# Block-sparse attention with a maxout layer: v brought into the query-tile layout by engine copies instead of DMAs inside the chip

## The chip, the cores and the metric

The kernel runs on one NeuronCore of a Trainium2 chip. Its engines are TensorE (PE; its weight loads are listed as PEld), VectorE (DVE), ScalarE (ACT), GpSimd (POOL) and SyncE (SP, which issues the DMAs). The metric is the device time of one execution in microseconds. Three runs of the kernel before took 192.92, 193.31 and 194.15 us, so the median is 193.31.

## What is computed

```python
# B, H, S, D = 4, 8, 768, 64; block = 32, window = 16, nb = 24
k_sum = k.reshape(B, H, nb, block, D).max(axis=3)
v_sum = v.reshape(B, H, nb, block, D).mean(axis=3)
scores_l = scale * q @ k.T, kept where |i - j| < window     # local keys
scores_s = scale * q @ k_sum.T + log(block)                 # block keys
a = softmax(concat([scores_l, scores_s]))
attn = a @ concat([v, v_sum])                               # per batch and head
x = attn, heads side by side                                # 3072 x 512
out = maximum(x @ w1, x @ w2) @ w_out                       # d_ff = 1024
```

All inputs and the output are fp32; the matmuls run in bf16.

## The kernel before

The work of a batch is eight heads, taken as four pairs (hp), and 768 queries, taken as three groups (grp) of 256. The queries are cut into twelve tiles of 64. A query tile meets 128 keys only: 64 + 32 local keys around it and the 24 block keys (with fillers). So there is, for every query tile, a row block of values in `vx` (128 partitions x 12 tiles x 8 heads x 66): partitions 0 to 63 and 96 to 127 hold the 96 rows of v near the tile, partitions 64 to 95 hold the block means, the same in all twelve tiles, and column 64 holds ones, from which the softmax's sum comes.

How v gets into `vx` (`load_v`, lines 276 to 333) is what the change touches. v of one batch arrives in two DMAs of four heads each, as fp32, in `vf` (two buffers, 128 rows x 4 heads x 6 row blocks x 64). POOL casts each half to bf16 in `vb` (one buffer, L340 by way of the helper `copy`, labelled "cast v"). Five pieces move rows of `vb` to their partitions and tiles of `vx`: two of 64 partitions (even and odd tiles) and three of 32. In batches 1 to 3 all five are DMAs from SP (L304); in batch 0 the two large pieces are DVE copies (L340) and the three small ones DMAs. PE makes the block means by six matmuls of `amean` with `vb` (L313), DVE copies them into tile 0 of `vx` (L319), and a DMA from `vx` to `vx` spreads them to the other eleven tiles (L327). The ones travel along with the rows, since `vb` is 66 wide. The load of v for a batch is issued only when the copies of the batch before are issued (`behind`).

The rest of attention: k and q are loaded, cast (k on DVE, or POOL for three pairs of batch 0; q on ACT), turned by PE (L359) and placed (k by DVE L373 into `kx`, with the block maximum L375, the wrap L379 and the spread of the sums L382; q by ACT L388 into `qx`). PE computes scores (L414, in batch 0 with the mask added by L403), ACT takes the exponential into `pb` (L426), DVE multiplies by the mask in batches 1 to 3 (L435, L441), PE computes the values (L460: `pb` with `vx`), DVE divides (L472, L474), PE turns the result (L484) and DVE copies it to `xt` (L489).

The maxout layer uses max(a, b) = a + relu(b - a): DVE makes w2 - w1 (`wd`, L506), POOL casts w1 (`w1b`), PE turns it (L516) and multiplies it with w_out once (L544, `w1o`), so that for each group of 256 queries PE computes the hidden part (L560, relu by ACT L565), the linear part (L574) and the product of the hidden part with w_out (L581). ACT copies the result out (L340) and SP stores it.

The order on each engine is not written by hand. Every operation is recorded with its engine, an assumed cost, its inputs and buffers and a priority. `Plan.run` plays the whole kernel through with these costs and lets each engine take the ready operation of the highest priority. The order that results is then fixed: an engine waits in that order. A change of a cost or of a buffer therefore also moves operations that are not edited. `vx` has two buffers, taken in turn by batch 0, the turned w1 (`w1t`), and batches 1, 2 and 3.

Of the kernel before, what the change touches and what calls it, by code (L numbers as in the profile page):

```python
# [13 lines left out]
BF16 = mybir.dt.bfloat16  # L14
# [114 lines left out]
def kernel(  # L129
# [14 lines left out]
    nc = tc.nc  # L144
# [64 lines left out]
    def fixed_parts():  # L209
# [36 lines left out]
        def make_amean():  # L246

            nc.gpsimd.memset(amean[:], 0.0)
            am = amean[:, :, 64:64 + nb]
            nc.gpsimd.memset(am, 1.0 / block)  # L250
            for base, mult, pat in ((0, 1, [[128, NM], [-block, nb]]),
                                    (block - 1, -1, [[-128, NM], [block, nb]])):
                nc.gpsimd.affine_select(out=am, in_=am, compare_op=ALU.is_ge, fill=0.0, base=base,
                                        channel_multiplier=mult, pattern=pat)
            for t in vbr.slots:
                nc.gpsimd.memset(t[:, :, :, D:VW], 1.0)

# [15 lines left out]

    v_spread = {-1: []}

    def load_v(b, prio, engines):

        vb = Buf(vbr)
        for n in range(2):
            f = Buf(vfr)  # L280
            op("SP", 3.55, lambda f=f, n=n: nc.sync.dma_start(
                out=f.ap[:].rearrange("p h m d -> p (h m) d"),
                in_=v[b, 4 * n:4 * n + 4].rearrange("h (m r) d -> r (h m) d", r=128)),
               write=[f], behind=v_spread[b - 1], prio=prio, label=f"load v{b}{n}")
            copy(engines[n], 1536, lambda f=f, n=n: (
                vb.ap[:, :, 4 * n:4 * n + 4, 0:D].rearrange("p m h d -> p h m d"), f.ap[:]),
                 read=[f, amean_in], write=[vb], prio=prio + 1, label=f"cast v{b}{n}")

        def rows(t):
            return t.rearrange("p t h w -> p t (h w)")  # L290

        last = []
        for piece, (lo, hi, tiles_, part, ms) in enumerate((
                (0, 64, slice(0, NT, 2), 0, slice(0, NM)),
                (0, 64, slice(1, NT, 2), 64, slice(0, NM)),
                (96, 128, slice(0, NT, 2), 64, slice(0, NM)),
                (96, 128, slice(1, NT - 1, 2), 0, slice(1, NM)),
                (96, 128, slice(NT - 1, NT), 0, slice(0, 1)))):
            aps = lambda lo=lo, hi=hi, tiles_=tiles_, part=part, ms=ms: (
                rows(vx[b].ap[lo:hi, tiles_]), rows(vb.ap[part:part + hi - lo, ms]))  # L300
            kw = dict(read=[vb], write=[vx[b]], prio=prio + 2, label=f"spread v{b}{piece}")
            if engines[2][piece] == "SP":
                last.append(op("SP", (1.7, 1.6, 1.0, 0.85, 0.3)[piece], lambda aps=aps: (
                    lambda o, i: nc.sync.dma_start(out=o, in_=i))(*aps()), **kw))  # L304
            else:
                e = engines[2][piece]
                copy(e, 0, aps, us=(1, 1, 1, 5 / 6, 1 / 6)[piece] * {
                    "DVE": 1.75, "ACT": 2.4, "POOL": 3.1}[e], **kw)
        ps, s, mean = Buf(banks, "mm"), slice(64, 96), Buf(Ring([None]))

        def means():
            for m in range(NM):
                nc.tensor.matmul(out=bank(ps), lhsT=amean[:, m, :], rhs=vb.ap[:, m, :, 0:D],  # L313
                                 start=(m == 0), stop=(m == NM - 1))
# [8 lines left out]
        def spread_means():  # L323
            o, i = rows(vx[b].ap[s, 1:NT]), rows(vx[b].ap[s, 0:1])
            i = i.to_broadcast([32, NT - 1, H * VW])
            if engines[3] == "SP":
                nc.sync.dma_start(out=o, in_=i)  # L327
            else:
                nc.vector.tensor_copy(out=o, in_=i)

        t = op(engines[3], 1.5 if engines[3] == "SP" else 2.0, spread_means, read=[mean],
           write=[vx[b]], prio=prio + 2, label=f"spread means {b}")
        v_spread[b] = [*last, t] if engines[3] == "SP" else last

# [264 lines left out]
    FIRST = (("DVE", "ACT"), ("POOL", "ACT"), ("POOL", "ACT"), ("POOL", "ACT"))  # L599
    FIRST_SPREAD = ("DVE", "DVE", "SP", "SP", "SP")  # L600

# [23 lines left out]
    V0 = 0.5  # L625
    load_v(0, V0, ("POOL", "POOL", FIRST_SPREAD, "SP"))
    for hp in range(1, NP):
# [48 lines left out]
```

## Time and profile before

| what | value |
|---|---|
| median of three runs | 193.31 us (192.92 to 194.15) |
| span of the profiled execution | 192.5 us |
| PE busy | 166.4 us (86%) |
| DVE, ACT, POOL busy | 109.9 (57%), 114.1 (59%), 25.7 us (13%) |
| DMA queue 1 | 37.01 MB, 71.8% of 16 engines |
| DMAs vx<-vb | 18, median 7.8 us from issue to landing |
| mean granted clock of TensorE | 0.991 |

The page names a group of instructions by its line, engine, operation and tiles, with "x" and a count, then its busy time and the mean duration in ns, then the idle time of the engine just before these instructions and what ended it. In the timeline a row begins with the start and the duration in us; rows of several instructions are merged. A line can be that of a helper: L340 is every cast or copy recorded by `copy`, so the tile names tell what it is. The chain is the work that ended last, followed back from the end; it passes DMAs until 70 us and, but for 82 to 97 us, PE from there on.

### The profile page before, as it was taken

To read this page: it belongs to the slowest core of one execution; us is meant where nothing else is said; L and a number is where in the kernel's file an instruction comes from. 1 tells how busy PE (TensorE), PEld (TensorE's weight loads), DVE (VectorE), ACT (ScalarE), POOL (GpSimd) and SP (SyncE) were. 2 spreads that over 40 slices of the span, in tenths; PEclk is the share of its full clock that TensorE was granted. 3 is DMA by queue.
4 is the path that set the end of the run, shared out by engine and by line. 5 is a ranking of instruction groups with operands and counts; after the bars stand their busy time and mean duration, and the time that the engine had idled before them with its cause. 6 is when DMAs were issued, how large, how long until landed. Compare 5 with 4: busy or idle time off the path is not lost.

```text
span 192.5 us, 4148 instructions
## 1 busy us (share of the span) xinstructions
PE 166.4 (86%) x1643; PEld 117.9 (61%) x1664; DVE 109.9 (57%) x289; ACT 114.1 (59%) x173; POOL 25.7 (13%) x39
## 2 busy tenths in 40 slices
PE   0629619899999969999979999999999999999990
PEld 0426419865757738758657767487696676665740
DVE  6908956888979438759868953079777600000000
ACT  2533964384689949219967955179986443342621
POOL 7556221300330003300003300000000000000000
PEclk9999996999999999999999999999999999999999
DMA  5999999999999999999999996061020111120303
GB/s 187 226 305 356 234 240 347 371 381 281 210 359 251 292 268 217 339 309 217 229 288 223 340 218 193 3 164 24 3 109 5 54 58 59 50 109 0 112 0 109
DMA packets 47859, 37.27 MB, mean 194 GB/s; under 512 B 26208, under 2 KB 43744, under 8 KB 47840
## 3 DMA queue, kind: packets, MB, share of 16 engines
q1 hardware_dynamic: 47840, 37.01, 71.8%
q8 instruction: 13, 0.21, 0.5%
q14 instruction: 6, 0.05, 0.1%
HBM read 25.17 MB, written 6.29 MB: 163 GB/s over the span
## 4 chain that ended last, share of the span: by engine, by line
PE 53%; DMA 33%; SPq 5%; DVE 4%; POOL 2%; issue 1%; ACT 0%; ACTq 0%
PE banks L581 17%; PE banks L560 16%; DMA vf<-in_v_dram 13%; DMA vx<-vb 10%; PE banks L574 7%; PE banks L460 5%; DMA wf<-in_moe_w_out_dram 4%; SPq L503 4%; DMA vx<-vx 4%; PE banks L414 3%; DMA kqf<-in_k_dram 2%; PE banks L359 2%; POOL vb L340 2%; PE banks L484 2%; PE banks L313 1%; DVE pb L435 1%
## 5 line engine op out<-in xcount | busy, mean ns | idle before, releaser
L560 PE MATMUL banks<-xt,wd 128*128 128x256 bf16 x384 | 46.6, 273 | 0.5 <-DVE xt L489 0.5
L581 PE MATMUL banks<-wo,g 128*128 128x512 bf16 x184 | 44.9, 379 | 0.4
L560 PEld LDWEIGHTS <-wd 128*128 128x128 bf16 x384 | 36.4, 98 | 6.1 <-issue 0.7
L426 ACT ACTIVATE pb<-banks,bias 128x512 bf16<-128x512 f32 x48 | 31.5, 686 | 10.2 <-PE banks L414 9.9
L565 ACT ACTIVATE g<-banks 128x512 bf16<-128x512 f32 x48 | 28.3, 596 | 13.7 <-PE banks L560 13.2
L340 ACT COPY o<-banks 128x512 f32<-128x512 f32 x24 | 14.0, 585 | 28.7 <-PE banks L581 28.4
L388 ACT COPY qx<-banks 64x768 bf16<-64x768 bf16 x32 | 25.3, 791 | 6.1 <-PE banks L359 5.8
L581 PEld LDWEIGHTS <-g 128*128 128x128 bf16 x192 | 17.2, 97 | 16.5
L460 PE MATMUL banks<-vx,pb 128*128 128x65 bf16 x384 | 19.4, 196 | 3.6 <-DMA vx<-vx 1.8
L574 PE MATMUL banks<-w1o,xt 128*128 128x512 bf16 x85 | 21.9, 379 | 0.6
L460 PEld LDWEIGHTS <-pb 128*128 128x128 bf16 x384 | 16.9, 100 | 7.1 <-DMA vx<-vx 2.1
L359 PE MATMUL banks<-identity,kqb 128*128 128x128 bf16 x192 | 16.6, 234 | 5.3 <-DVE kqb L340 4.7
L340 ACT CAST kqb<-kqf 128x768 bf16<-128x768 f32 x16 | 13.1, 830 | 13.6 <-DMA kqf<-in_q_dram 8.7
L414 PE MATMUL banks<-qx,kx 128*128 128x128 bf16 (+2 forms) x208 | 18.6, 226 | 2.3 <-ACT qx L388 1.3
L340 POOL CAST vb<-vf 128x1536 bf16<-128x1536 f32 x8 | 12.2, 1520 | 55.0 <-DMA vf<-in_v_dram 35.2
L474 DVE TENSOR_TENSOR xs<-banks,inv 128x256 bf16<-128x256 f32 x48 | 19.1, 415 | 0.3
L414 PEld LDWEIGHTS <-kx 128*128 128x128 bf16 x208 | 15.1, 103 | 6.6 <-DVE kx L382 2.4
L359 PEld LDWEIGHTS <-kqb 128*128 128x128 bf16 x192 | 13.6, 106 | 8.5 <-DVE kqb L340 4.7
L373 DVE COPY kx<-banks 128x768 bf16<-128x768 bf16 x16 | 15.2, 955 | 2.9 <-PE banks L359 1.7
L375 DVE TENSOR_REDUCE ks<-kx 128x24 bf16<-128x768 bf16 x16 | 15.1, 944 | 0.1
L489 DVE COPY xt<-banks 128x512 bf16<-128x512 bf16 x24 | 9.8, 418 | 7.2 <-PE banks L484 6.8
L574 PEld LDWEIGHTS <-xt 128*128 128x128 bf16 x96 | 8.9, 98 | 7.9
(47 smaller groups left out, 129.8 us busy)
## 6 DMA issues: line engine op xcount, KB each, us to landing
kqf<-in_k_dram SPq DMA_DIRECT2D x16, 384.0 KB, 6.6
kqf<-in_q_dram SPq DMA_DIRECT2D x16, 384.0 KB, 5.7
vf<-in_v_dram SPq DMA_DIRECT2D x8, 768.0 KB, 10.7
out_dram<-o SPq DMA_DIRECT2D x20, 256.0 KB, 2.2
wf<-in_moe_w_dram SPq DMA_DIRECT2D x8, 512.0 KB, 11.1
vx<-vb SPq DMA_DIRECT2D x6, 396.0 KB, 8.0
wf<-in_moe_w_out_dram SPq DMA_DIRECT2D x4, 512.0 KB, 8.6
vx<-vx SPq DMA_DIRECT2D x4, 363.0 KB, 6.2
```

The source lines that it names most:

```text
L340: {"DVE": nc.vector.tensor_copy, "ACT": nc.scalar.copy, "POOL": nc.gpsimd.tensor_copy}[engine](out=o, in_=i)
L359: nc.tensor.transpose(out=bank(ps, S, BF16)[:, 128 * j:128 * j + 128], in_=src.ap[:, j].rearrange("p h d -> p (h d)"), identity=identity[:])
L373: op("DVE", 0.96, lambda: nc.vector.tensor_copy(out=kt()[:, :, 0:64], in_=order(kps)), read=[kps], write=[kx[b, hp], kmain], prio=prio, la ...
L388: op("ACT", 0.8, lambda a=a, r=r: nc.scalar.copy(out=qx[b, hp].ap[r, a, :], in_=order(qps)[r]), read=[qps], write=[qx[b, hp]], prio=prio, ...
L414: nc.tensor.matmul(out=o[:, :, n0:n1], lhsT=w, rhs=qx[b, hp].ap[:, :, c:c + n1 - n0], start=(mask_on != "PE"), stop=(mask_on != "PE" or (i ...
L426: op("ACT", 0.7, lambda: nc.scalar.activation(out=pv(), in_=bank(ps).rearrange("p (i w q) -> p i w q", w=2, q=64), func=ACT.Exp, bias=bias ...
L460: nc.tensor.matmul(out=av()[:, u, a, :], lhsT=pb.ap[:, 2 * u + a, 64 * par:64 * par + 128], rhs=vx[b].ap[:, 4 * grp + 2 * u + par, 2 * hp ...
L474: op("DVE", 0.42, lambda: nc.vector.tensor_tensor(out=x.ap[:, hp % 2], in0=av()[:, :, :, 0:D], in1=inv.ap[:].to_broadcast([128, 2, 2, D]), ...
L560: nc.tensor.matmul(out=bank(ps)[:, 256 * s:256 * s + 256], lhsT=wd[n].ap[:, c, 128 * s:128 * s + 128], rhs=x.ap[:, c, :], start=(c == 0), ...
L565: op("ACT", 0.6, lambda n=n, ps=ps: nc.scalar.activation(out=g.ap[:, 2 * n:2 * n + 2, :].rearrange("p f n -> p (f n)"), in_=bank(ps), func ...
L574: nc.tensor.matmul(out=bank(ps), lhsT=x.ap[:, c, sl], rhs=w1o[c].ap[:], start=(c == 0), stop=False)
L581: nc.tensor.matmul(out=bank(ps), lhsT=g.ap[:, f, sl], rhs=wo[f // 2].ap[:, f % 2, :], start=False, stop=(f == FC - 1))
```

## The change

The DMAs inside the chip go. `vb` becomes 64 wide and serves the means alone. Every piece is now an engine's cast from the fp32 `vf` into `vx`, per half of the heads, so ten pieces a batch in place of five. In batches 1 to 3 all ten are on POOL. In batch 0 DVE has five and POOL the other five. The ones are set by one POOL memset over all of `vx`. The means are spread by one DVE copy (32 partitions x 88 x 64), in all batches. The loads of v are no longer held behind the copies. In the new kernel's numbering lines are some 12 lower: L328 is the helper, L347 the turns, L304 the means, L310 their copy, L316 their spread, L402 the scores, L423 and L429 the masks, L448 the values, L548, L562 and L569 the maxout layer.

```diff
-    vbr = Ring(tiles("vb", 1, [128, NM, H, VW], BF16))
+    vbr = Ring(tiles("vb", 1, [128, NM, H, D], BF16))
...
-    def load_v(b, prio, engines):
+    def load_v(b, prio, casts, spreads, stretch):
 
         vb = Buf(vbr)
+
+        def piece(f, n, engine, to, of, tag, **kw):
+            aps = lambda: (vx[b].ap[to[0], to[1], 4 * n:4 * n + 4, 0:D].rearrange("p t h d -> p h t d"),
+                           f.ap[of[0], :, of[1], :])
+            count = 4 * D * len(range(NM)[of[1]])
+            copy(engine, 0, aps, us=0.1 + count * {"DVE": 0.00056, "ACT": 0.00102, "POOL": 0.00097}[engine],
+                 read=[f, *kw.pop("also", [])], write=[vx[b]], prio=prio + 1, label=f"spread v{b}{n}{tag}")
+
+        lo, hi, top, tail = slice(0, 64), slice(64, 128), slice(96, 128), slice(0, 32)
+        every = slice(0, NM)
...
-               write=[f], behind=v_spread[b - 1], prio=prio, label=f"load v{b}{n}")
+               write=[f], prio=prio, label=f"load v{b}{n}")
...
+            e = spreads[n]
+            piece(f, n, e[0], (lo, slice(0, NT, 2)), (lo, every), 0)
+            piece(f, n, e[1], (lo, slice(1, NT, 2)), (hi, every), 1)
+            piece(f, n, e[2], (top, slice(0, NT, 2)), (slice(64, 96), every), 2)
+            piece(f, n, e[3], (top, slice(1, NT - 1, 2)), (tail, slice(1, NM)), 3)
+            piece(f, n, e[3], (top, slice(NT - 1, NT)), (tail, slice(0, 1)), 4)
...
-        op("POOL", 0.1, lambda: nc.gpsimd.memset(vx[b].ap[s, 0, :, D:VW], 1.0),
-           write=[vx[b], mean], prio=prio, label=f"ones {b}")
+        op("POOL", 1.0, lambda: nc.gpsimd.memset(vx[b].ap[:, :, :, D:VW], 1.0),
+           write=[vx[b]], prio=prio, label=f"ones {b}")
...
+        def spread_means(lo, hi):
+            eng = nc.vector
+            eng.tensor_copy(out=vx[b].ap[s, lo:hi, :, 0:D], in_=vx[b].ap[s, 0:1, :, 0:D].to_broadcast(
+                [32, hi - lo, H, D]))
...
-    load_v(0, V0, ("POOL", "POOL", FIRST_SPREAD, "SP"))
+    load_v(0, V0, ("POOL", "POOL"), (("DVE", "DVE", "POOL", "POOL"), ("DVE", "DVE", "DVE", "POOL")), ((1, NT),))
...
-        load_v(b, 1000 * b - 480, ("POOL", "POOL", ("SP",) * 5, "SP"))
+        load_v(b, 1000 * b - 480, ("POOL", "POOL"), (("POOL",) * 4,) * 2, ((1, NT),))
```

Three places of the order matter below. The first is POOL in the prelude, from the arrival of the first half of v (`vf_92`) to the first weight cast. Before:

```order
L340 CAST vb_94<-vf_92 128x4x6x64
L340 CAST vb_94<-vf_93 128x4x6x64
L340 CAST kqb_70<-kqf_64 128x2x6x64
L340 CAST kqb_68<-kqf_66 128x2x6x64
L340 CAST kqb_69<-kqf_62 128x2x6x64
L340 CAST w1b_128<-wf_116 128x1024
```

And now:

```order
L328 CAST vb_94<-vf_92 128x4x6x64
L328 CAST vx_95<-vf_92 32x4x6x64
L328 CAST vx_95<-vf_92 32x4x5x64
L328 CAST vx_95<-vf_92 32x4x64
L328 CAST kqb_70<-kqf_64 128x2x6x64
L328 CAST vb_94<-vf_93 128x4x6x64
L328 CAST vx_95<-vf_93 32x4x5x64
L328 CAST vx_95<-vf_93 32x4x64
L328 CAST kqb_68<-kqf_66 128x2x6x64
L328 CAST kqb_70<-kqf_62 128x2x6x64
L328 CAST w1b_128<-wf_116 128x1024
```

Five casts into `vx` stand among the casts of k for pairs 1 to 3 (`kqb`), and one of these now comes ahead of the second half of v.

The second place is DVE in the prelude. Before, from the two copies of v to the placing of the last k (`kx_75`, the fourth pair):

```order
L340 COPY vx_95<-vb_94 64x6x528 x2
L373 COPY kx_73<-banks 128x12x64
L319 CAST vx_95<-banks 32x8x64
L375 TENSOR_REDUCE ks_98<-kx_73 128x24
L379 COPY kx_73<-kx_73 128x32
L382 COPY kx_73<-ks_98 128x12x24
L373 COPY kx_74<-banks 128x12x64
L373 COPY kx_75<-banks 128x12x64
```

And now, where two casts from `vf_92` stand five memsets ahead of the first row:

```order
L328 CAST vx_95<-vf_93 64x4x6x64 x2
L328 CAST vx_95<-vf_93 32x4x6x64
L361 COPY kx_73<-banks 128x12x64
L363 TENSOR_REDUCE ks_98<-kx_73 128x24
L367 COPY kx_73<-kx_73 128x32
L370 COPY kx_73<-ks_98 128x12x24
L310 CAST vx_95<-banks 32x8x64
L316 COPY vx_95<-vx_95 32x88x64
L361 COPY kx_74<-banks 128x12x64
```

Five casts stand in place of two copies, and the spread of the means (`32x88x64`) is new on DVE, ahead of the placing of the third k.

The third place is POOL at the beginning of batch 1, where `vx_95` is taken over from batch 0. Before, between the last weight cast and the casts of batch 2:

```order
L340 CAST w1b_131<-wf_122 128x1024
L317 MEMSET vx_95 32x8x2
L317 MEMSET vx_96 32x8x2
L340 CAST vb_94<-vf_92 128x4x6x64
L340 CAST vb_94<-vf_93 128x4x6x64
```

And now, up to the memset for batch 2:

```order
L328 CAST w1b_131<-wf_122 128x1024
L308 MEMSET vx_95 128x96x2
L328 CAST vb_94<-vf_92 128x4x6x64
L328 CAST vx_95<-vf_92 64x4x6x64 x2
L328 CAST vx_95<-vf_92 32x4x6x64
L328 CAST vx_95<-vf_92 32x4x5x64
L328 CAST vx_95<-vf_92 32x4x64
L328 CAST vb_94<-vf_93 128x4x6x64
L328 CAST vx_95<-vf_93 64x4x6x64 x2
L328 CAST vx_95<-vf_93 32x4x6x64
L328 CAST vx_95<-vf_93 32x4x5x64
L328 CAST vx_95<-vf_93 32x4x64
```

Two casts have become twelve, behind a memset that waits until batch 0's values no longer read `vx_95`. Batches 2 and 3 have the same row of twelve.

More of the change, by code (lines that the diff above doesn't have):

```diff
@@ L283, in load_v @@
                 in_=v[b, 4 * n:4 * n + 4].rearrange("h (m r) d -> r (h m) d", r=128)),
-               write=[f], behind=v_spread[b - 1], prio=prio, label=f"load v{b}{n}")
-            copy(engines[n], 1536, lambda f=f, n=n: (
-                vb.ap[:, :, 4 * n:4 * n + 4, 0:D].rearrange("p m h d -> p h m d"), f.ap[:]),
+               write=[f], prio=prio, label=f"load v{b}{n}")
+            copy(casts[n], 1536, lambda f=f, n=n: (
+                vb.ap[:, :, 4 * n:4 * n + 4, :].rearrange("p m h d -> p h m d"), f.ap[:]),
                  read=[f, amean_in], write=[vb], prio=prio + 1, label=f"cast v{b}{n}")
[L289 to L308, printed above, removed]
+            e = spreads[n]
[4 more added lines that the diff above has]
+            piece(f, n, e[3], (top, slice(NT - 1, NT)), (tail, slice(0, 1)), 4)
         ps, s, mean = Buf(banks, "mm"), slice(64, 96), Buf(Ring([None]))
@@ L321, in load_v @@
            read=[ps], write=[vx[b], mean], prio=prio + 2, label=f"means {b}")
[L323 to L333, printed above, removed]
+        def spread_means(lo, hi):
+            eng = nc.vector
+            eng.tensor_copy(out=vx[b].ap[s, lo:hi, :, 0:D], in_=vx[b].ap[s, 0:1, :, 0:D].to_broadcast(
+                [32, hi - lo, H, D]))
+        for lo_, hi_ in stretch:
+            op("DVE", 0.12 + (hi_ - lo_) * 0.15, lambda lo_=lo_, hi_=hi_: spread_means(lo_, hi_), read=[mean],
+               write=[vx[b]], prio=prio + 2, label=f"spread means {b}")
     RATE = {"DVE": 0.00068, "ACT": 0.00102, "POOL": 0.00095}
```

6 lines of the change are left out of this document (1 added, 5 removed).

## The prediction

> **What bounds the kernel now.** I read the 40 slices first, then the busy times by stage, then what TensorE waits for, then the rows around each wait.
>
> ```profile
> PE   0629619899999969999979999999999999999990
> DVE  6908956888979438759868953079777600000000
> ```
>
> ```profile
> 9.00:30.00 21.00, 11.74 (x108) 8.65 (x106) 12.44 (x22) 11.62 (x16) 8.21 (x7) 0.98 1.11 287
> 30.00:45.00 15.00, 14.09 (x198) 11.51 (x197) 12.41 (x36) 8.97 (x12) 2.19 (x3) 0.91 1.07 367
> 45.00:100.00 55.00, 51.12 (x530) 35.94 (x538) 41.15 (x99) 37.86 (x58) 6.26 (x6) 1.00 1.09 270
> ```
>
> The columns are the stretch, its length, the busy time of PE, PEld, DVE, ACT and POOL with instruction counts, the granted clock, the DMA share and GB/s. From 30 us on PE is the bound. The prelude is different: between 9 and 30 us PE is busy for 11.7 of 21 us, and the DMA engines are full (share 1.11, and still 1.09 up to 100 us). So the change can act in three places: the prelude, the moments when PE stands for the copied v, and wherever the engines that take over the copying become late. DVE is at 75% between 45 and 100 us, POOL at 11%.
>
> PE's waits for copied v are two:
>
> ```profile
> 70.42 0.63 PE L460 MATMUL banks<-vx,pb 128*128 128x65 bf16 x15 [1.75 <-DMA vx<-vx]
> 97.36 0.61 PE L460 MATMUL banks<-vx,pb 128*128 128x65 bf16 x15 [1.30 <-DMA kqf<-in_k_dram]
> 91.95 0.61 SPq L327 DMA_DIRECT2D vx<-vx  x1
> vx<-vx SPq DMA_DIRECT2D x4, 363.0 KB, 6.2
> ```
>
> Both are the first values matmuls of a batch. The second names a k load, but the instruction reads only vx and pb. The spread of the means was issued at 91.95, and such a DMA lands in 6.2 us (median), so that is the real releaser. No wait on batch 3's copies is listed.
>
> **What goes: 3.05 us.** All 18 vx<-vb and 4 vx<-vx DMAs are removed, and with them both waits, 1.75 + 1.30, provided that vx is now ready in time (below). In the prelude 396 KB of vx<-vb and 363 KB of vx<-vx leave a full queue. At the 287 GB/s of that stretch this is 2.7 us by which the weight loads can land sooner. Whether this helps is decided by what PE waits for next.
>
> **What comes: POOL and DVE copy, and they block each other.** The prices:
>
> ```profile
> L340 POOL CAST vb<-vf 128x1536 bf16<-128x1536 f32 x8 | 12.2, 1520 | 55.0 <-DMA vf<-in_v_dram 35.2 <-PE banks L460 19.8
> L340 POOL CAST w1b<-wf 128x1024 bf16<-128x1024 f32 x4 | 4.2, 1040 | 14.3 <-DMA wf<-in_moe_w_dram 14.3
> L340 DVE CAST kqb<-kqf 128x768 bf16<-128x768 f32 x13 | 7.6, 586 | 1.5 <-DMA kqf<-in_k_dram 1.5
> L340 DVE COPY vx<-vb 64x3168 bf16<-64x3168 bf16 x2 | 2.6, 1276 | 4.7 <-POOL vb L340 4.7
> L382 DVE COPY kx<-ks 128x288 bf16<-128x288 bf16 x16 | 3.7, 229 | 0.0
> L379 DVE COPY kx<-kx x16: 136/164/1025, 7.4 to 145.4; 128x32 bf16<-128x32 bf16 x16
> L435 DVE TENSOR_TENSOR pb<-pb,mask x24: 390/416/1637, 54.0 to 149.3; 128x512 bf16<-128x512 bf16 x24
> L506 DVE TENSOR_TENSOR wd<-wf,wf 128x1024 bf16<-128x1024 f32 x4 | 4.9, 1222 | 0.8 <-DMA wf<-in_moe_w_dram 0.8
> ```
>
> A POOL cast of 1536 elements takes 1.47 us undisturbed (rows below) and one of 1024 takes 1.04, so 0.84 ns an element: 1280 elements 1.26, 768 elements 0.83, 256 elements 0.4. No row shows POOL moving data to other partitions or using half of them. I take the same price and bound it above by twice that (a rival). One half of v costs POOL 4 x 1.47 + 1.26 + 0.4 = 7.5 us, a batch 15.1, against 2.9 before. DVE casts 1536 fp32 elements in twice 0.586 less one fixed part of 0.16, that is 1.0. Spreading the means is 88 x 64 = 5632 elements. By the step from L379 (32 elements, 0.164) to L382 (288, 0.229) it takes 1.6, by the 3168-element copy 2.3; I take 1.75, near the first since it is also a broadcast copy.
>
> These engines get in each other's way:
>
> ```profile
> 50.34 1.47 POOL L340 CAST vb<-vf 128x1536 bf16<-128x1536 f32 x1 [2.71 <-DMA vf<-in_v_dram]
> 54.12 1.64 POOL L340 CAST vb<-vf 128x1536 bf16<-128x1536 f32 x1 [2.31 <-DMA vf<-in_v_dram]
> 75.54 1.47 POOL L340 CAST vb<-vf 128x1536 bf16<-128x1536 f32 x1 [19.78 <-PE banks L460]
> 78.89 1.47 POOL L340 CAST vb<-vf 128x1536 bf16<-128x1536 f32 x1 [1.89 <-DMA vf<-in_v_dram]
> 103.21 1.47 POOL L340 CAST vb<-vf 128x1536 bf16<-128x1536 f32 x1 [22.64 <-DMA vf<-in_v_dram]
> 106.50 1.70 POOL L340 CAST vb<-vf 128x1536 bf16<-128x1536 f32 x1 [1.83 <-DMA vf<-in_v_dram]
> ```
>
> ```profile
> 50.81 1.02 DVE L379 COPY kx<-kx 128x32 bf16<-128x32 bf16 x1
> 55.13 1.04 DVE L340 CAST kqb<-kqf 128x768 bf16<-128x768 f32 x1 [0.70 <-DMA kqf<-in_k_dram]
> 56.43 0.48 DVE L441 TENSOR_TENSOR pb<-pb,mask 128x256 bf16<-128x256 bf16 x2
> 75.75 1.60 DVE L441 TENSOR_TENSOR pb<-pb,mask 128x256 bf16<-128x256 bf16 x2
> 103.31 1.64 DVE L435 TENSOR_TENSOR pb<-pb,mask 128x512 bf16<-128x512 bf16 x1
> 107.13 1.42 DVE L441 TENSOR_TENSOR pb<-pb,mask 128x256 bf16<-128x256 bf16 x2
> ```
>
> Each of these slow DVE instructions begins inside a POOL cast and ends just after it: the copy at 50.81 takes 1.02 instead of 0.16 and ends at 51.83, the cast at 51.81. Against their usual 0.16, 0.59, 0.48, 0.42 and 0.48 the excesses are 0.86, 0.45, 1.12, 1.22 and 0.94, together 4.6 us for six POOL casts of 9.2 us in the attention stages: 0.5 us of DVE per us of POOL. DVE instructions that read PSUM show no such excess.
>
> The Trainium skill has this as a rule (SBUF — State Buffer, Who interferes with whom): VectorE and GpSimd share one port pair, whoever starts first keeps it for the whole instruction, and the other one blocks fully. It speaks against this change. The rows agree (1.02 against 0.16), and if by this rule every such instruction met a cast the time would be that of the second rival.
>
> **Prelude, +2.2 us.**
>
> ```profile
> 9.25 1.47 POOL L340 CAST vb<-vf 128x1536 bf16<-128x1536 f32 x1 [1.84 <-DMA vf<-in_v_dram]
> 14.13 0.83 POOL L340 CAST kqb<-kqf 128x768 bf16<-128x768 f32 x1
> 15.88 1.59 POOL L340 CAST kqb<-kqf 128x768 bf16<-128x768 f32 x1 [0.92 <-DMA kqf<-in_k_dram]
> 17.96 0.83 POOL L340 CAST kqb<-kqf 128x768 bf16<-128x768 f32 x1 [0.48 <-DMA kqf<-in_k_dram]
> 14.24 2.72 PE L313 MATMUL banks<-vb,amean 128*128 128x512 bf16 x6 [3.37 <-POOL vb L340]
> 20.60 1.82 DVE L373 COPY kx<-banks 128x768 bf16<-128x768 bf16 x2
> 24.45 0.23 DVE L382 COPY kx<-ks 128x288 bf16<-128x288 bf16 x1
> 28.64 0.62 PE L516 MATMUL banks<-identity,w1b 128*128 128x128 bf16 x8 [3.98 <-POOL w1b L340]
> 37.26 0.62 PE L516 MATMUL banks<-identity,w1b 128*128 128x128 bf16 x8
> 161.99 3.49 PE banks L560 x32
> ```
>
> From 9.25 us POOL now has ten casts up to the last k (3 x 1.47 + 2 x 1.26 + 2 x 0.4 + 3 x 0.83 = 10.2) and DVE five v casts (5.0). One after the other they end at 24.5; before, the last k cast ended at 18.8. The second means input is cast at about 20.8; the means at the cold pace of 2.72 end at 23.5, their copy at 24.2. The spread waits for a w1b cast until 25.4 and ends at 27.2, and in DVE's order it stands ahead of the placing of the third and fourth k. Those two took 4.1 us before (20.60 to 24.68); with two small instructions between them they end at 32.0 instead of 24.7. Then DVE needs four wd (4 x 1.22) and some twelve small ones, net 7.9, until the first x is transposed: 39.9. The amount of PE work up to a place is the number of matmuls in the order by their pace at full clock (32 of L560 in 3.49 us in the chain, the others by their columns in the same way). In the old run PE had done 13.8 us of work at 37.26, so the 14.2 that now stand ahead of the first L548 were done at 37.7. So PE is 2.2 us late, although its wait of 3.98 at 28.64 for a weight is gone: that gain of the freed DMA has no taker. Unhindered, the same chain has 24.8 us of DVE work from 9.3, so 34.1: this end is kept for the first rival.
>
> **Batch 1: vx in time.** POOL may start when batch 0's last values are done, 4.9 us of PE work later: 44.8. With 0.3 for the ones, 15.1 for the casts and some 2.3 us lost to DVE it ends at 62.5. PE's order has 24.6 us of matmuls from 39.9 to the first values of batch 1: 64.5. There is no wait, by a margin of 2 us; before, 30 us of matmuls stood between these two places, and PE still waited 1.75. Batches 2 and 3 follow at about 83 and 100, PE asks at about 94 and after 120. The v loads need buffers that POOL frees late, but each lands in some 10 us while POOL works on the other half.
>
> **Later stages, +2.0 us.**
>
> ```profile
> L460 PE MATMUL banks<-vx,pb 128*128 128x65 bf16 x384 | 19.4, 196 | 3.6 <-DMA vx<-vx 1.8 <-DMA kqf<-in_k_dram 1.3 <-DVE pb L435 0.5
> ```
>
> POOL's added 3 x 12 = 36 us cost DVE 18 us at 0.5. Of the 4.6 us lost in the old run PE felt 0.5, all of it behind a mask of L435 (the one of 103.31), so 11%: 2.0 us. The lower end is zero, if every stall falls where a tile is not wanted soon. The upper end is that one stall by itself: of 1.2 us it passed on 0.5, that is 42%, or 7.6 us.
>
> **Sum** for the profiled execution of 192.5: - 3.05 + 2.2 + 2.0 gives 193.65. The median of the runs is 0.8 above that span, so I forecast **194.4 us**, which is within 1% of before.
>
> **Rivals.**
>
> First, faster: the casts interleave without lengthening the chain. DVE stands idle for 4.7 us ahead of its copies of v (the group row of vx<-vb), and fills that gap now. The prelude then ends 3.6 us earlier (34.1 against 37.7), weights that land 2.7 us sooner carry it, and the later stages cost half, 1.0: 192.5 - 3.05 - 3.6 + 1.0 + 0.8 = 187.7. Against it stands that the 15.88 cast took 1.59 beside a DVE copy of v instead of 0.83: the gap is shared.
>
> Second, slower: masks late on DVE. In batches 2 and 3 PE comes back for a masked tile soon after its scores, so a DVE that stalls at every mask holds PE in its fixed order. It decides once the stalls exceed that slack; at the 42% of 103.31 the later stages cost 7.6: 192.5 - 3.05 + 2.2 + 7.6 + 0.8 = 200.0. Against it stands DVE's idle quarter, which absorbs part.
>
> Third, the copying does not keep up: POOL's moved partitions cost double, nine us more a batch, and vx of batch 1 is ready at 71.5 instead of 62.5. PE waits 7 us there, the wait that was to be removed: 201.4.
>
> **Chances.** Forecast 0.37, first rival 0.30, second 0.25, third 0.08. Faster than before by over 1% (about what a measurement of this kernel can tell from no change) is the first rival, 0.30; within 1% 0.35, which is the forecast less a small part past 195.2; slower 0.35. The range runs from the first rival to the second, 187.5 to 200; the forecast alone would span 191.5 to 197.
>
> **What would show it.** Right: no wait of L448 on vx; DVE copies and masks of over 1 us beside POOL casts, about 18 us in all; the third and fourth k placed near 32 us and the first L548 near 40. Wrong: the first L548 before 36 (first rival); waits of PE on masks summing to over 5 us (second); POOL casts on 64 partitions well over 1.5 us with DVE idle (third).

## The result: 206.74 us, slower by 6.4%

| | before | after |
|---|---|---|
| median (range) | 193.20 (192.92 to 194.15), 4 runs | 206.74 us (204.34 to 207.63), 4 runs |
| ratio, 95% interval | | 1.064 [1.0552, 1.0728] |
| span of the profiled execution | 192.5 | 202.6 us (its own time 204.34, the lowest of the four) |
| DVE busy | 109.9 (57%) | 137.1 us (68%) |
| POOL busy | 25.7 (13%) | 71.1 us (35%) |
| PE busy | 166.4 (86%) | 168.1 us (83%) |
| DMA queue 1 | 37.01 MB, 71.8% | 31.46 MB, 53.0% |

The forecast was 194.4 in a range to 200; the time lies beyond the range. Some executions show a slower state, here the one of 207.63 us; the ratios, and the differences to the changed kernel below, leave these out (its median is then 206.25). The work of PE is the same. The 40 slices of the changed kernel's page show where it stands idle:

```profile
PE   0614986699995268999969999999899999999992
DVE  7899799996999999664999866219988652000000
POOL 7699840019996995019990000000000000000000
PEclk9999999999999769999999999999999999999998
```

A slice is 5.1 us. The 13th and 14th (61 to 71 us) are the new hole: PE falls to 5 and 2, DVE stands at 9, and the granted clock falls to 7 and 6 in the 14th and 15th. Two stretches of the changed kernel, with the columns of the prediction's (PE, PEld, DVE, ACT, POOL, granted clock, DMA share, GB/s):

```profile
45.00:60.00 15.00, 14.88 (x118) 9.08 (x119) 13.18 (x19) 9.59 (x15) 14.63 (x11) 1.00 0.91 263
60.00:80.00 20.00, 11.54 (x122) 8.71 (x122) 19.85 (x28) 8.64 (x14) 16.74 (x15) 0.83 0.57 147
```

Between 60 and 80 us DVE is busy for 19.85 of 20 us and finishes only 28 instructions. PE is busy for 11.54 us of it. The DMA share, which was over 1 up to 100 us before, is 0.57. So the queue is relieved, which the change was for, and a new bound has come: DVE. PE's waits say what it stands for (us in total, times, longest):

```profile
PE banks L347 <- POOL kqb L328: 6.3, 1, 6.3
PE banks L347 <- DVE kqb L328: 5.3, 3, 4.7
PE banks L402 <- DVE kx L370: 4.7, 3, 3.7
PE banks L448 <- DVE vx L316: 3.3, 2, 2.3
PE banks L448 <- DVE xs L462: 2.2, 1, 2.2
PE banks L448 <- DVE pb L423: 1.5, 1, 1.5
```

The two longest, 6.3 and 4.7 us, are the prelude's waits for keys; the run without the casts, below, has them too (6.4 and 4.6) and takes 193.49. New in the middle are the wait for `kx` (3.7 at one place), that for `xs` (2.2) and that of batch 1 for the spread of the means (2.3; the other 1.0 is batch 0's). Just there the chain of waits runs through DVE almost without a break:

```profile
62.93 3.08 DVE vx L316
66.04 3.09 DVE pb L423 x2
69.12 1.21 DVE kx L370
70.33 2.40 DVE kqb L328 x2
72.73 2.97 DVE pb L429 x2
```

The last four rows are seven instructions: two masks of 512, the spread of the sums, two casts of k, two masks of 256. By their usual 0.42, 0.23, 0.59 and 0.28 they need 2.8 us; they took 9.7 (66.04 to 75.70). The timeline of the changed kernel shows why, POOL first, then DVE. A short cast and a cast of k, from 70.2 on, are left out:

```profile
65.78 1.46 POOL L328 CAST vx<-vf 64x1536 bf16<-64x1536 f32 x1
67.29 1.56 POOL L328 CAST vx<-vf 32x1536 bf16<-32x1536 f32 x1
68.89 1.34 POOL L328 CAST vx<-vf 32x1280 bf16<-32x1280 f32 x1
70.65 1.68 POOL L328 CAST vb<-vf 128x1536 bf16<-128x1536 f32 x1
72.27 1.78 POOL L328 CAST vx<-vf 64x1536 bf16<-64x1536 f32 x1
74.09 1.46 POOL L328 CAST vx<-vf 64x1536 bf16<-64x1536 f32 x1
```

```profile
66.04 1.49 DVE L423 TENSOR_TENSOR pb<-pb,mask 128x512 bf16<-128x512 bf16 x1
67.45 1.68 DVE L423 TENSOR_TENSOR pb<-pb,mask 128x512 bf16<-128x512 bf16 x1
69.05 1.28 DVE L370 COPY kx<-ks 128x288 bf16<-128x288 bf16 x1
70.92 1.81 DVE L328 CAST kqb<-kqf 128x768 bf16<-128x768 f32 x1
72.66 1.54 DVE L429 TENSOR_TENSOR pb<-pb,mask 128x256 bf16<-128x256 bf16 x1
74.12 1.58 DVE L429 TENSOR_TENSOR pb<-pb,mask 128x256 bf16<-128x256 bf16 x1
```

Each DVE instruction begins 0.03 to 0.39 us after a POOL cast and ends 0.10 to 0.40 us after its end. The next cast has begun by then, and the next DVE instruction finds it there. With work queued on both sides they take turns, one for one, and DVE moves at the pace of one instruction per POOL cast.

### The profile page after: what moved, and what is told of

It reads as the page before. It is cut to its first block, busy times and chain, and to the rows that moved or that the text cites. A ratio compares the mean times of both kernels' runs of the same rounds, so it can differ in the third digit from the quotient of the medians.

```text
span 202.6 us, 4162 instructions
## 1 busy us (share of the span) xinstructions
PE 168.1 (83%) x1644; PEld 118.0 (58%) x1664; DVE 137.1 (68%) x296; ACT 112.6 (56%) x173; POOL 71.1 (35%) x73
## 3 DMA queue, kind: packets, MB, share of 16 engines
q1 hardware_dynamic: 42240, 31.46, 53.0%
## 4 chain that ended last, share of the span: by engine, by line
PE 58%; DVE 25%; issue 6%; POOL 5%; DMA 3%; SPq 0%; ACT 0%; DVEq 0%; ACTq 0%
PE banks L569 17%; PE banks L548 15%; PE banks L562 8%; PE banks L448 5%; DVE kqb L328 4%; DVE kx L361 4%; DMA vf<-in_v_dram 3%; DVE ks L363 3%; DVE vx L316 3%; PE banks L402 3%; DVE pb L423 3%; PE banks L532 3%; PE banks L304 3%; PE banks L472 2%; DVE pb L429 2%
## 5 line engine op out<-in xcount | busy, mean ns | idle before, releaser
L548 PE MATMUL banks<-xt,wd 128*128 128x256 bf16 x384 | 47.8, 276 | 0.4 <-DVE vx L310 0.2
L569 PE MATMUL banks<-wo,g 128*128 128x512 bf16 x186 | 45.2, 379 | 0.3
L328 POOL CAST vx<-vf 64x1536 bf16<-64x1536 f32 (+3 forms) x35 | 44.1, 1270 | 1.1
L548 PEld LDWEIGHTS <-wd 128*128 128x128 bf16 x384 | 36.9, 99 | 6.7 <-issue 0.6
L328 ACT COPY o<-banks 128x512 f32<-128x512 f32 x24 | 14.0, 585 | 34.0 <-PE banks L569 31.2
L376 ACT COPY qx<-banks 64x768 bf16<-64x768 bf16 x32 | 25.3, 790 | 10.7 <-PE banks L347 10.4
L347 PE MATMUL banks<-identity,kqb 128*128 128x128 bf16 x192 | 16.6, 234 | 13.0 <-POOL kqb L328 6.3
L569 PEld LDWEIGHTS <-g 128*128 128x128 bf16 x192 | 17.2, 97 | 16.6
L448 PE MATMUL banks<-vx,pb 128*128 128x65 bf16 x384 | 19.0, 194 | 7.0 <-DVE vx L316 3.3
L402 PE MATMUL banks<-qx,kx 128*128 128x128 bf16 (+2 forms) x208 | 18.4, 227 | 6.2 <-DVE kx L370 4.7
L347 PEld LDWEIGHTS <-kqb 128*128 128x128 bf16 x192 | 13.4, 105 | 16.1 <-POOL kqb L328 6.4
L448 PEld LDWEIGHTS <-pb 128*128 128x128 bf16 x384 | 16.6, 98 | 10.2 <-issue 5.8
L562 PE MATMUL banks<-w1o,xt 128*128 128x512 bf16 x84 | 21.9, 379 | 0.6
L402 PEld LDWEIGHTS <-kx 128*128 128x128 bf16 x208 | 15.0, 104 | 10.2 <-DVE kx L370 7.3
L328 ACT CAST kqb<-kqf 128x768 bf16<-128x768 f32 x16 | 12.9, 829 | 9.1 <-DMA kqf<-in_q_dram 6.0
L423 DVE TENSOR_TENSOR pb<-pb,mask 128x512 bf16<-128x512 bf16 x24 | 14.0, 601 | 2.6 <-ACT pb L414 2.6
L328 POOL CAST vb<-vf 128x1536 bf16<-128x1536 f32 x8 | 13.7, 1716 | 4.3 <-DMA vf<-in_v_dram 3.3
```

What stands on the lines that cost most here:

```text
L328: {"DVE": nc.vector.tensor_copy, "ACT": nc.scalar.copy, "POOL": nc.gpsimd.tensor_copy}[engine](out=o, in_=i)
L347: nc.tensor.transpose(out=bank(ps, S, BF16)[:, 128 * j:128 * j + 128], in_=src.ap[:, j].rearrange("p h d -> p (h d)"), identity=identity[:])
L376: op("ACT", 0.8, lambda a=a, r=r: nc.scalar.copy(out=qx[b, hp].ap[r, a, :], in_=order(qps)[r]), read=[qps], write=[qx[b, hp]], prio=prio, ...
L402: nc.tensor.matmul(out=o[:, :, n0:n1], lhsT=w, rhs=qx[b, hp].ap[:, :, c:c + n1 - n0], start=(mask_on != "PE"), stop=(mask_on != "PE" or (i ...
L448: nc.tensor.matmul(out=av()[:, u, a, :], lhsT=pb.ap[:, 2 * u + a, 64 * par:64 * par + 128], rhs=vx[b].ap[:, 4 * grp + 2 * u + par, 2 * hp ...
L548: nc.tensor.matmul(out=bank(ps)[:, 256 * s:256 * s + 256], lhsT=wd[n].ap[:, c, 128 * s:128 * s + 128], rhs=x.ap[:, c, :], start=(c == 0), ...
```

## The experiments

**Theory.** POOL's casts hold up DVE for the length of a whole POOL instruction each time, and since both have queues, DVE falls behind until PE waits. **Rivals:** the spread of the means on DVE costs it; the order that the planner found is bad by itself; the values come late because POOL copies slowly.

All twelve kernels, with the ratio to the kernel before on the same chip:

| kernel | median us | ratio, 95% interval |
|---|---|---|
| changed order, no POOL casts into vx in batches 1 to 3 | 193.49 | 1.0046 [1.0001, 1.0092] |
| changed order, no spread of means in batches 1 and 3 | 202.17 | 1.0491 [1.0416, 1.0565] |
| these casts on ACT | 207.42 | 1.0753 [1.0679, 1.0828] |
| before with 14 more POOL casts in each of batches 1 to 3 | 195.99 | none (192.44 to 196.3) |
| changed order, memsets for the casts | 201.88 | 1.0454 [1.0412, 1.0497] |
| before, means spread by DVE in batches 1 to 3 | 193.63 | 1.0006 [0.9965, 1.0046] |
| the same in all batches | 194.49 | 1.0063 [1.0010, 1.0117] |
| changed order, casts in halves | 202.51 | 1.0493 [1.0448, 1.0537] |
| changed order, casts only in batch 1 (and 0) | 197.54 | 1.0194 [1.0111, 1.0277] |
| changed order, casts only in batch 3 (and 0) | 195.56 | 1.0141 [1.0073, 1.0208] |
| changed order, casts in quarters | 195.53 | 1.0131 [1.0075, 1.0188] |
| quarters everywhere, spread in three, planned anew | 192.18 | 0.9934 [0.9894, 0.9974] |

"Changed order" means that each engine keeps the changed kernel's order but for the edit. Where casts or spreads are left out, `vx` holds older values there; with memsets, zeros. Line numbers shift by a few in these kernels: the mask of 512 is L423 to L431, the spread L316 to L321.

### The casts or the spread?

Without the casts of batches 1 to 3 (a POOL memset in the prelude, not shown, fills a part of the second `vx`, which would be unwritten):

```diff
-            copy(engine, 0, aps, us=...
+            copy(engine, 0, (lambda: None) if b else aps,
+                 us=...
```

> The changed kernel with the same order on every engine, but POOL's casts into vx are left out in batches 1 to 3 (the output then uses older values there); everything else stays, the cast for the means and the spread of the means by DVE too. Blocking theory (POOL's casts and DVE's SBUF copies and masks exclude each other): DVE's masks fall back to a median and a largest time of about 0.42 and 0.28 us, TensorE's stall between 60 and 80 us goes but for about 2 us behind the spread of the means, and the time falls by 5 to 8 us to 198 to 201. Added-work theory (the 3.08 us spreads and the other DVE work delay what stands behind them): the time stays within 2 us of 206. Order theory (the new fixed order is too tight for any lateness): it stays above 203.

Measured: 193.49 us, 12.8 less than the changed kernel and more than the 5 to 8 that I expected. Its row for the stretch of the hole, and the one wait on vx that is left, in the prelude:

```profile
60.00:80.00 20.00, 19.35 (x238) 14.91 (x237) 16.94 (x44) 15.46 (x26) 3.30 (x2) 1.00 1.04 257
...
PE banks L456 <- DVE vx L321: 1.9, 1, 1.9
```

Within this order the casts are the whole loss; the planner's order by itself loses nothing that can be told from no change. Batch 1 does not wait for the spread here, so that wait of 2.3 us is the casts' work too. The order also gains nothing: with most of POOL's copying free of charge the time is that of before.

Without the spread of the means in two batches:

```diff
         def spread_means(lo, hi):
+            if b in (1, 3):
+                return
```

> The changed kernel with the same order, but DVE's spread of the means is left out in batches 1 and 3 (the means of batch 0 stay in those tiles), POOL's casts all stay. Blocking theory: only the 2.3 us wait of the values on the spread and a part of what stands behind it go, so minus 2 to 3 us, 203 to 204. Added-work theory: the stall of batch 1 was made by it, so minus 5 us or more, 201 or less.

Measured: 202.17 us, so 4.1 less for two copies of together 6.2 us, between the two expectations. One of the copies stood in the hole (62.93), the other at 137.47, behind the last cast; which of them brought how much was not told apart. Alone the spread costs nothing, as two kernels show that are the one before with only the spread put on DVE (the diff is the first's; the second does the same in batch 0):

```diff
-        load_v(b, 1000 * b - 480, ("POOL", "POOL", ("SP",) * 5, "SP"))
+        load_v(b, 1000 * b - 480, ("POOL", "POOL", ("SP",) * 5, "DVE"))
```

> One part of the change alone: the kernel before, its DMAs from vb to vx kept, but the means of batches 1 to 3 spread by DVE (32 partitions x 5808, rows of 528 with the ones). The two waits of the values on the DMA from vx to vx (1.75 and 1.30 us) go; DVE pays 1.7 us (if these long rows run at the pace of the 3168-element copies) to 3.2 us (at the pace of the change's spread) three times. Blocking theory: this part is harmless, 190 to 193. Added-work theory: the spread delays the masks behind it, 194 or more.

> As the run with DVE spreading the means of batches 1 to 3, and in batch 0 too. That takes 363 KB more out of the full DMA queue of the prelude (some 1.3 us) and puts 1.7 to 3.2 us on DVE ahead of the third k. Blocking theory: within 1 us of the other one. Added-work theory: slower than the other one by 1 to 2 us.

Measured: 193.63 and 194.49 us, beside 193.53 of the kernel before. The first does away with both waits of before on the copied means (1.75 and 1.30), and it brings nothing. In its profiled execution a wait of another kind stands later:

```profile
114.42 0.41 PE L460 MATMUL banks<-vx,pb 128*128 128x65 bf16 x8 [1.71 <-DVE pb L435]
113.94 0.42 DVE L435 TENSOR_TENSOR pb<-pb,mask 128x512 bf16<-128x512 bf16 x1 [3.82 <-ACT pb L426]
111.88 0.83 ACT L340 CAST kqb<-kqf 128x768 bf16<-128x768 f32 x1 [3.96 <-DMA kqf<-in_q_dram]
```

PE's wait names a mask, but DVE had stood idle for 3.82 us until the exponential came, and ACT, whose order has a cast of q ahead of it, for 3.96 until the q load landed. So the 3.05 us that the prediction took off were not to be had in full: next behind the vx that is now in time, a load of q was late.

### What in a POOL cast does it?

The same copying on ACT, planned anew with ACT's cost:

```diff
-        load_v(b, 1000 * b - 480, ("POOL", "POOL"), (("POOL",) * 4,) * 2, ((1, NT),))
+        load_v(b, 1000 * b - 480, ("POOL", "POOL"), (("ACT",) * 4,) * 2, ((1, NT),))
```

> The changed kernel with ScalarE in place of POOL for the casts into vx in batches 1 to 3; the planner makes a new order for it. Blocking theory: DVE's masks take their usual 0.42 and 0.28 us beside these casts, and unless ScalarE (113 us busy, now some 157) becomes the bound the time is under 201. Added-work theory: the DVE work is the same, so it stays near 206. If ScalarE is the bound, TensorE's waits name exponentials and relus, and the time says nothing on the other two.

Measured: 207.42 us. One row tells that DVE is free, two that another bound has come (a late stretch, and the wait that it holds):

```profile
L423 DVE TENSOR_TENSOR pb<-pb,mask x24: 394/424/664, 64.1 to 161.9; 128x512 bf16<-128x512 bf16 x24
```

```profile
125.00:150.00 25.00, 17.00 (x191) 13.38 (x190) 19.58 (x45) 23.74 (x32) 0.00 (x0) 0.80 0.01 2
...
PE banks L402 <- ACT qx L376: 7.3, 2, 6.0
```

The longest mask takes 0.66 us in place of 1.68, so it is POOL that holds up DVE and not the copying. But ACT, at 23.74 of 25 us, delivers q late and PE stands. A free engine for this work is not there.

POOL memsets of the same regions in place of the casts of batches 1 to 3:

```diff
+            if engine == "POOL0":
+                nc.gpsimd.memset(o, 0.0)
+                return
```

> The changed kernel in the same order, with each POOL cast into vx in batches 1 to 3 replaced by a POOL memset of the same elements (v is left out there, the values come out as zero sums but for the means). POOL is about as long busy, but only writes. If DVE is blocked through the read side alone, everything on DVE is free and the time falls to that without POOL's casts, 193 to 195. If a DVE mask (two inputs in SBUF) is blocked only by a POOL instruction that reads, and a DVE cast or copy by both, masks return to 0.42 and 0.28 us while casts of k still take up to 1.8, and the time comes between, 195 to 201. If POOL's being busy is enough, whatever it does, the time stays near 206.

Measured: 201.88 us. DVE's rows by form, first of this kernel, then of the changed one:

```profile
L331 DVE CAST kqb<-kqf 128x768 bf16<-128x768 f32 x13 | 14.7, 1146 | 0.1
L426 DVE TENSOR_TENSOR pb<-pb,mask 128x512 bf16<-128x512 bf16 x24 | 10.4, 449 | 2.6 <-ACT pb L417 2.6
L373 DVE COPY kx<-ks 128x288 bf16<-128x288 bf16 x16 | 6.8, 423 | 0.0
L432 DVE TENSOR_TENSOR pb<-pb,mask 128x256 bf16<-128x256 bf16 x24 | 5.8, 280 | 0.3 <-ACT pb L417 0.2
```

```profile
L423 DVE TENSOR_TENSOR pb<-pb,mask 128x512 bf16<-128x512 bf16 x24 | 14.0, 601 | 2.6 <-ACT pb L414 2.6
L328 DVE CAST kqb<-kqf 128x768 bf16<-128x768 f32 x13 | 11.2, 874 | 0.1
L429 DVE TENSOR_TENSOR pb<-pb,mask 128x256 bf16<-128x256 bf16 x24 | 9.6, 439 | 0.3 <-ACT pb L414 0.2
L370 DVE COPY kx<-ks 128x288 bf16<-128x288 bf16 x16 | 4.6, 289 | 0.0
L367 DVE COPY kx<-kx 128x32 bf16<-128x32 bf16 x16 | 4.5, 279 | 0.0
```

Beside memsets the masks run at their usual 0.45 and 0.28, but the casts and copies are held up more than beside casts (1146 and 423 against 874 and 289 ns). The Trainium skill states just this (SBUF — State Buffer, Who interferes with whom): an instruction with two SBUF inputs meets only those of GpSimd that read, a copy or cast of DVE in a two-port mode meets any. The trace agrees on both halves. For the time it matters little which instruction is held up: 8.4 us of the 12.8 remain with the masks free.

### Where in the kernel, and how long an instruction?

Casts in one of the batches 1 to 3 only (the diff is for batch 1):

```diff
-            copy(engine, 0, (lambda: None) if b else aps,
+            copy(engine, 0, (lambda: None) if b in (2, 3) else aps,
```

> The changed kernel's order with POOL's casts into vx only in batches 0 and 1; those of batches 2 and 3 are left out, so their values are computed with stale v. If the casts cost where PE needs masked tiles and new keys within a few us (after 60 us; by PE's work offset the old and new kernel were only 1.0 us apart at batch 1's first values, and 8 by 93 us), the casts of batch 1, which run from 45 to 61, are cheap: 194 to 196.5. If each batch's casts cost a like share of the 13 us that all three cost: 198.

> The same with the casts into vx only in batches 0 and 3; those of batches 1 and 2 are left out, so their values are computed with stale v. By the offsets of PE's work batch 3's casts (90 to 107) cost about 2: 195.5. With a like share for each batch: 198. If with this and the run for batch 1 alone less than 6 of the 13 us are found, most of it belongs to batch 2's casts (63 to 79) or to casts that follow on each other.

Measured: 197.54 and 195.56 us, against 193.49 with none: 4.1 for batch 1 and 2.1 for batch 3. The first expectation, that batch 1's casts are cheap, was wrong: 197.54 is near the 198 of a like share. Together they are 6.1 of 12.8, so 6.6 belong to batch 2's casts or to casts that meet a DVE that is late already; these two were not told apart.

Every cast into vx split in two, and in four, one head each, nothing else changed:

```diff
+            if engine == "POOL2":
+                for h in range(4):
+                    nc.gpsimd.tensor_copy(out=o[:, h], in_=i[:, h])
+                return
```

> The changed kernel in the same order, with each POOL cast into vx in batches 1 to 3 split into two of two heads each (768, 640 and 128 elements). Nothing is left out. If a DVE instruction waits for the rest of the one POOL instruction that is under way, its wait halves (masks beside casts at most about 1.2 us instead of 1.7) and the time falls by 3 to 6 us, to 201 to 203, although POOL takes some 15% longer. If POOL's total busy time counts, or the fixed order, it stays at 206 or rises.

> The changed kernel with every POOL cast into vx of batches 1 to 3 split into four, one head each. Splitting in two took 4.2 us off. If what counts is that a DVE instruction waits for the rest of one POOL instruction, a further halving of its length (0.48 by 0.84 ns an element and a fixed part) takes another 1 to 3 us off: 199.5 to 201.5, with masks of at most 0.9. If what counts is POOL's total time, which grows by the fixed part of each instruction: 203 to 205.

Measured: 202.51 and 195.53 us. The quarters take 10.7 of the 12.8 us off, far more than the 5 to 7 that I expected, though POOL now works longer for the same elements: in the kernel with quarters, the first row below gives 0.54 us a quarter, 2.2 a piece in place of 1.47. The other rows are the seven DVE instructions that took 9.7 us, and what PE waits for `kx`:

```profile
L330 POOL CAST vx<-vf 64x384 bf16<-64x384 f32 x48 | 24.2, 543 | 0.3
```

```profile
64.29 1.01 DVE L427 TENSOR_TENSOR pb<-pb,mask 128x512 bf16<-128x512 bf16 x2
65.22 0.48 DVE L374 COPY kx<-ks 128x288 bf16<-128x288 bf16 x1
65.63 1.09 DVE L332 CAST kqb<-kqf 128x768 bf16<-128x768 f32 x2
66.64 0.55 DVE L433 TENSOR_TENSOR pb<-pb,mask 128x256 bf16<-128x256 bf16 x2
```

```profile
60.00:80.00 20.00, 19.00 (x226) 14.41 (x225) 18.74 (x44) 14.81 (x25) 19.64 (x42) 1.00 0.85 226
...
PE banks L406 <- DVE kx L374: 1.9, 3, 0.8
```

They take 2.9 us (64.29 to 67.19), and DVE does 44 instructions between 60 and 80 us in place of 28. POOL is busier there than ever (19.64 of 20 us), and it costs little. So what DVE pays is not POOL's total time but the length of the one POOL instruction that it has to wait for, and the rival of the late values falls: POOL ends batch 1's casts at 67.0 here, 6 us later than in the changed kernel, and PE waits for none of them. The few long ones left, the inputs of the means at 1.46, still show: the longest mask of 512, 1.15 us at 77.84, met one of them (77.25).

### Is it the casts in any order?

The kernel before with 14 POOL casts of 1024 elements that nobody reads, in each of batches 1 to 3:

```diff
+    def extra():
+        for _ in range(14):
+            nc.gpsimd.tensor_copy(out=w1b[3].ap[:], in_=wfr.slots[5])
```

> The kernel before in its own order, with 14 added POOL casts of 1024 elements (1.04 us each, from a weight buffer that is done with to another one) behind the second v cast of batches 1 to 3; nobody reads what they write, the output is the reference's. Blocking theory: DVE's masks beside them take up to 1.5 us and the time rises by 3 to 7 us, to 196 to 200, less than the change's since batch 1's masks are wanted late in this order. Added-work and order theories: nobody waits for these casts, so the time stays at 193.

Measured: 192.44, 195.96, 196.02 and 196.3 us. Only the first can be set beside the kernel before, and one run gives no ratio; it shows no cost, where I had expected 196 to 200, and by the others the casts cost at most some 3 us. DVE was held up as in the changed kernel (execution of 195.96 us): the median mask of 512 took 0.53 us, the longest 1.70, and DVE was busy for 121.1 us in place of 109.9. That speaks for the order of before having more room for late DVE work than the changed one. It is a hint and not shown, as these casts are of 1.09 us, and at other times.

### A version that beats both?

POOL's casts of v in quarters everywhere, the inputs of the means too; the spread of batches 1 to 3 in three copies; the planner given the measured costs:

```diff
-            copy(casts[n], 1536, lambda f=f, n=n: (
+            copy("POOL2", 1536, us=2.0, aps=lambda f=f, n=n: (
...
-        load_v(b, 1000 * b - 480, ("POOL", "POOL"), (("POOL",) * 4,) * 2, ((1, NT),))
+        load_v(b, 1000 * b - 480, ("POOL", "POOL"), (("POOL",) * 4,) * 2, ((1, 4), (4, 8), (8, NT)))
```

> A try at a version that beats both kernels: all POOL casts of v, batch 0 and the inputs of the means too, in quarters; the spread of the means of batches 1 to 3 in three DVE copies that the planner may place apart; the planner given the measured costs (1.4 ns an element for the quarters, 0.27 us a tile for the spread), so the order is another than the changed kernel's. If exclusion by long POOL instructions was the whole of the loss, what is left over the old kernel (195.5 against 193.3) is the spread and the prelude, and this gives 191.5 to 194. If the order that the planner finds matters as much, anything from 192 to 197; and a time at or above 195.5 means that nothing was left to gain there.

Measured: 192.18 us (191.87 to 193.74) beside 194.08 of the kernel before on that chip, ratio 0.9934 [0.9894, 0.9974]: the fastest of all, by less than the 1% that I said a measurement can tell from no change. Behind 42 us the trace names no wait of PE at all. The longest mask takes 0.78 us. The spread in three:

```profile
L316 DVE COPY vx<-vx 32x2048 bf16<-32x2048 bf16 x6 | 5.0, 864 | 0.0
L316 DVE COPY vx<-vx 32x1536 bf16<-32x1536 bf16 x3 | 2.8, 944 | 0.1
```

How much of it is the cuts and how much the new order was not separated.

## Why the prediction was wrong

On the spans, 192.5 and 202.6, the prediction's terms against what the traces give:

| step | forecast | measured |
|---|---|---|
| waits on copied v | -3.05 | -3.05 for the DMAs, +2.25 for batch 1's spread |
| prelude | +2.2 | +0.6 |
| later stages | +2.0 | +10.3, the rest |
| sum | +1.15 | +10.1 |

The run without the casts has a span of 191.8, so the casts cost 10.8, the 2.25 of batch 1's spread among them. Without them 0.7 is gained out of the 3.05. Of the other 2.4 the prelude explains 0.6; the rest stays open and is within the spread of that kernel's executions (spans of 190.1 to 192.6).

**The step that failed is "Later stages, +2.0 us", and in it the 11%.** The blocked time itself was put too high: by the group rows of the changed kernel shown above, less the usual durations, DVE lost (601 - 424) x 24 + (439 - 283) x 24 + (874 - 586) x 13 + (289 - 229) x 16 + (279 - 164) x 16 ns = 14.5 us. The same sum gives 3.8 in the kernel before and 4.2 without the casts, so the casts added about 10.5, where I had 18. What was wrong by far more is how much of it reaches PE: not 11%, not the 42% of the upper end, but in this order nearly all. The busy times show it without that sum. All these kernels run the changed order with the same instructions on DVE, so what DVE is busy longer is blocking (both columns are of the profiled execution):

| kernel | DVE busy, us | span, us |
|---|---|---|
| without the casts | 125.9 | 191.8 |
| casts in batch 3 only | 129.3 | 195.5 |
| casts in batch 1 only | 129.8 | 196.0 |
| casts in quarters | 130.7 | 194.0 |
| memsets for the casts | 134.0 | 200.1 |
| casts in halves | 135.5 | 200.7 |
| changed kernel | 137.1 | 202.6 |

Against the first row the span grows by 0.9 to 1.1 us for each us that DVE is busy longer (10.8 for 11.2 in the changed kernel); by the medians it is 0.6 to 1.1. Only the quarters pass on less than half (2.2 for 4.8).

I had taken the share from single stalls of the old run, six POOL casts that stood alone, each behind a DVE that then had time to catch up. In the changed kernel twelve casts stand in a row, and DVE has little room: without the casts it is idle for 3.1 us between 60 and 80 (16.94 of 20 busy), and the seven instructions from 66.04 on lose 6.9 us in one piece. PE waited 3.71 for the third of them, the sums. "DVE's idle quarter, which absorbs part" was a mean over 55 us; between 60 and 80 of the changed kernel nothing was idle. That shorter stalls are caught up between, which would explain the quarters, is argued and not shown. Nor is it shown what in the order of before took in a DVE busy time of 11 us more for at most 3 us. Some of the loss is the clock: it was 0.83 between 60 and 80 in the changed kernel and 1.00 without the casts, which is worth up to 0.17 x 20 = 3.4 us. It fell after PE had begun to stand idle; its share of the loss was not measured apart.

**The second rival had the mechanism, and its size was off.** Masks late on DVE, PE held in its fixed order, slower: this is what came, though in batch 1 as well, where the rival had named batches 2 and 3. Its price of 7.6 at 42% was too low. Its own test would have missed it: I asked for more than 5 us of PE's waits on masks, and they are 1.5. In the hole PE's waits bear the name of what stood last in DVE's queue, the sums (3.7) and xs (2.2), not of the masks that were held up ahead of them.

**Prelude.** The first L548 came at 38.28, forecast 39.9; at equal PE work the old run was at 37.7. The spread of the means did not wait for POOL: it ran from 22.81 to 25.89, beside two casts of w1 (22.62 to 24.64). The fourth k was placed at 30.5, where I had 32.0. DVE's casts of v were dearer than I had them, 1.52 for 64 x 1536 (mean of four) in place of 1.0, and the spread of the means was, too, at 3.08 in place of 1.75.

```profile
22.81 3.08 DVE L316 COPY vx<-vx 32x5632 bf16<-32x5632 bf16 x1
38.28 1.04 PE L548 MATMUL banks<-xt,wd 128*128 128x256 bf16 x8
```

**vx in time.** POOL ended batch 1's casts at 61.0, forecast 62.5, and PE asked at 63.8, forecast 64.5. But vx is ready when the means are spread, too, and for that I had a price only in the prelude. It took 3.08 and not 1.75 us, began at 62.93 in a queue that was late, and PE waited 2.25:

```profile
66.06 0.61 PE L448 MATMUL banks<-vx,pb 128*128 128x65 bf16 x15 [2.25 <-DVE vx L316]
```

**The third rival fell.** POOL's casts to other partitions, and to fewer, cost what the straight ones cost: 1.46 for 64 x 1536 at 74.09, where the straight one had 1.47. The first rival fell as well: the prelude did not end earlier, and there was no gain to be carried on.

## What to carry to other kernels

Work that goes to POOL is paid for on DVE, and not by POOL's own time: where DVE has a row of copies, casts or products of two SBUF tiles queued, each of them waits out one whole POOL instruction, so look at DVE's load in that stretch and not at its mean. If POOL must copy there, cut its instructions until they are about as short as DVE's own; here quarters took more work on POOL and brought back 10.7 of 12.8 us. Between two kernels with the same instructions on DVE, a longer busy time of DVE shows the blocking, where PE's waits name only the last of a late row. And a wait that is removed is worth only the distance to the next thing that is late: two waits of together 3.05 us were worth nothing that could be measured.

## What the runs showed of the hardware

- With queues on both sides, DVE and POOL take turns instruction by instruction (the rows from 65.78 to 75.70). Neither gets two in a row there, as long as DVE's next is one of those that POOL holds up.
- The spread of the means is no such instruction: 3.08 us for 5632 elements, beside POOL casts and without them, 1.8 elements a ns. Cut to four tiles it takes 0.68 us undisturbed for 2048 elements (3.0 a ns, the row below, when POOL had ended) and 0.90 to 0.99 beside POOL's quarters; cut to three tiles it takes 0.94 for 1536 (1.6 a ns), the same at all three places.

```profile
127.98 0.68 DVE L316 COPY vx<-vx 32x2048 bf16<-32x2048 bf16 x1
```

  The Trainium skill has the condition (VectorE: DVE Perf Modes, Mode 2×_2P): both ports work on one tensor only if its outermost dimension is even, or odd and equal for source and destination. Here the source's is 11, 3 or 4 tiles, and the destination's is 8 times that, as its heads and tiles run on (the order lists the whole copy as 32x88x64). The trace agrees in all three cases. By this rule the copy of eleven tiles is of the slow kind, and one that does not meet POOL.
- A POOL cast takes about 0.84 ns an element and a fixed part, on 32, 64 or 128 partitions, moved or not: 1.04 us for 1024 elements and 1.47 for 1536 on 128, 1.46 for 1536 moved on 64. On 32 partitions 1536 took 1.46 as well, at 49.62.
